# An interleaved attention and token-mixer kernel: the last key block in two widths of columns, a query product moved into attention, and new turn lists

## The chip, the cores and the metric

The kernel runs on one core of a Trainium2 chip. The metric is the device time of one execution in microseconds, as the median of several runs. A core has these engines: TensorE (PE in the profile: matmuls; its weight loads are shown apart as PEld), VectorE (DVE), ScalarE (ACT), GpSimd (POOL) and SyncE (SP, which here issues the DMAs). Each engine takes its instructions in the order in which the program lists them, and waits at an instruction until the data that it needs have been written by the others. Matmuls write to PSUM, eight banks of 2 KB in each of 128 partitions; the other data lie in SBUF.

## The reference

```python
def _A_ref(x, wq, wk, wv, wo):          # S=2048, D=512, H=32, Dh=16
    q = (x @ wq).reshape(B, S, H, Dh).transpose(0, 2, 1, 3)
    k = x @ wk                          # one head of keys and values for all
    v = x @ wv
    scores = jnp.einsum("bhqd,bkd->bhqk", q, k) * (Dh ** -0.5)
    p = _softmax(scores, axis=-1)
    o = jnp.einsum("bhqk,bkd->bhqd", p, v)
    return o.transpose(0, 2, 1, 3).reshape(B, S, H * Dh) @ wo

def _B_ref(x, w1, b1, w2, b2):          # F=1792, the MLP runs along the tokens
    h = _layernorm(x, axis=-1)
    u = _gelu(jnp.einsum("bsd,sf->bdf", h, w1) + b1)
    y = jnp.einsum("bdf,fs->bds", u, w2) + b2
    return y.transpose(0, 2, 1)

x = A_x
x = x + _A_ref(_layernorm(x), A_wq, A_wk, A_wv, A_wo)
x = x + _B_ref(_layernorm(x), B_w1, B_b1, B_w2, B_b2)
x = x + _A_ref(_layernorm(x), A_wq, A_wk, A_wv, A_wo)
x = x + _B_ref(_layernorm(x), B_w1, B_b1, B_w2, B_b2)
```

Everything is float32. Products that need the precision are made of pairs: a number is split into a rounded part (type fp32r, "high") and the rest ("low"), and three matmuls of such parts stand for one.

## The kernel before

The program runs the two layers, 0 and 1, one behind the other; each is an attention and a token MLP. The 2048 tokens are 16 tiles of 128 (`x0` to `x15`) and four blocks of 512 (`b` = 0 to 3, four tiles each).

**Attention** goes through 32 groups. A group is four heads for one block of 512 queries; in layer 1 groups 0 to 7 belong to block 2. The scores of a group are 32 pairs: a pair is 128 keys against two heads, two matmuls of 512 columns into one two-bank PSUM tile `sc` (L909), and then one exponential over 128x1024 on ScalarE (L919). There are three `sc` tiles; a pair's tile comes free when its exponential has read it. To free it earlier, VectorE can copy a pair out of PSUM first (L917), and ScalarE then reads the copy (`p<-p` instead of `p<-sc`); such a pair is called copied here. The sums (`acc`, L925) are the matmuls of the exponentials with the values, four small ones for a pair. Below, 9.13 means pair 13 of group 9. The names in the code count differently: `sc_9_6_2` is group 9, key tile 6 (of 16, of 128 keys each), heads 2 and 3, so pair 13.

What TensorE does in what order during attention is set by lists of numbers, the **turns** (`WHOLE`, `LONG`, `COPIED`, `QUAD`, `QUAD_TO_FOUR` and so on, near the head of the file). A positive number issues the scores of that many pairs, the tens digit 1 (12, 13) marking that the last of them is copied; a negative number issues sums, so many pairs of them; a zero issues the next piece of other work: half a query product, a quarter of an output projection (`po`) or a product of the next MLP's first layer (`pu`). Work lies in a list that `later` makes (query products of later blocks, and the rows of their shifts), and in the Mixer, whose `turn` chooses lists for `po` and `pu`. A query product that finds enough room is given as a LONG turn of 16 pairs, otherwise as a WHOLE one of 12, so that what is put into the list early shifts where each later one falls. A **guard** (`proj.guard`, L627 in the profile) reads a flag, computed from bounds, and branches to a slow path that these data do not take; there is one in front of some groups, at which the engines stop for the branch.

**The entry of layer 1** is the code at the end of `tile_mqa_mixer_kernel`, behind layer 0's MLP, where no attention runs on any engine yet. `x` of the last block (tiles 12 to 15) is ready last. Its normalized tiles `h` are transposed by TensorE into `pt` (L386), split into high and low parts `hT` by ScalarE (`first_rows`, L397) and VectorE (`second_rows`, L401), and multiplied with the key and value weights into `pk` and, for block 2's queries, with `wq` into `pq` (both L415: `product` makes the generator of 12 matmuls, and `fill` issues so many of them). From `pk` come the squares `kk` (L457), `kg` (L449) and `kv` (L466) on ScalarE; from the squares, by a matmul with a column of ones (`pn`, L499), a maximum (`km`, L569), a diagonal (L571) and a matmul of that with ones (L573), the bound `kb` of the keys' norms (L576). It goes into row 0 of the keys, `kst`, in pieces (`bound_row`, L583), and the first scores need it. Each product of queries is put away in four steps: rounded (`round_queries`, L516, on ScalarE or VectorE), squared on GpSimd (`square_queries`, L524), subtracted to get the low part (`second_queries`, L528, VectorE), and stored to DRAM (`store_queries`, L533), from where the groups load it as `qs` (L788). `first_guard` issues the guard ahead of group 0; behind it `put` puts queries away between two steps of `bound_rows`, which writes the bound into the rest of `kst`.

In layer 1, before, the first three of block 2's four query products (0, 1, 2) are made in the entry, and only the fourth is left to `later`, as `project(NB - 2, [ND - 1])`.

## Time and profile before

| | us |
|---|---|
| median of 3 runs | 2517.36 |
| their lowest and highest | 2516.68, 2517.88 |
| the profiled execution | 2514.03 |
| its span in the trace | 2512.3 |
| PE busy | 2492.7 |
| ACT busy | 2102.8 |
| DVE busy | 1550.9 |
| POOL busy | 147.8 |

The page is of one execution. A row of its groups reads: line, engine, operation, out<-in with the tile's sizes and type, how many, then the busy time of all, the mean in ns of one, and the idle time of the engine ahead of them with what ended most of it. A row of the timeline begins with the start in us from the span's start and the time that the instructions of the row took together; in brackets stands the idle time ahead and what ended it. A row of the windows has a stretch, its length, the busy time of the engines asked for (instructions in brackets), the clock that TensorE was granted as a share of the full one, the share of the DMA engines' time and GB/s. Layer 0's exponentials run from 44.6 us to about 1041, layer 1's from 1296.3 to about 2289.

### The profile page before, as it was taken

To read this page: it belongs to the slowest core of one execution; us is meant where nothing else is said; L and a number is where in the kernel's file an instruction comes from. 1 tells how busy PE (TensorE), PEld (TensorE's weight loads), DVE (VectorE), ACT (ScalarE), POOL (GpSimd) and SP (SyncE) were. 2 spreads that over 40 slices of the span, in tenths; PEclk is the share of its full clock that TensorE was granted. 3 is DMA by queue.
4 is the path that set the end of the run, shared out by engine and by line. 5 is a ranking of instruction groups with operands and counts; after the bars stand their busy time and mean duration, and the time that the engine had idled before them with its cause. 6 is when DMAs were issued, how large, how long until landed. Compare 5 with 4: busy or idle time off the path is not lost. (4 is left out here: it accounts for less than half of the span.)

```text
span 2512.3 us, 41954 instructions
## 1 busy us (share of the span) xinstructions
PE 2492.7 (99%) x16158; PEld 1240.3 (49%) x16158; DVE 1550.9 (62%) x2458; ACT 2102.8 (84%) x2344; POOL 147.8 (6%) x235
## 2 busy tenths in 40 slices
PE   9999999999999999999999999999999999999999
PEld 6444334444444444588863443344444444445887
DVE  6565566667766776564445664666677667765522
ACT  6999999999999999653349999999999999995511
POOL 5000000000000000141000000000000000002200
PEclk9999999999999999999999999999999999999999
DMA  3221201111111111134423211111111111102343
GB/s 116 75 66 41 65 27 41 31 42 31 39 31 39 31 41 31 43 110 149 128 58 118 61 45 48 31 39 31 41 31 39 31 42 33 40 26 66 107 125 95
DMA packets 168679, 143.56 MB, mean 57 GB/s; under 512 B 17650, under 2 KB 132368, under 8 KB 167952
## 3 DMA queue, kind: packets, MB, share of 16 engines
q1 hardware_dynamic: 168464, 140.72, 19.3%
q8 instruction: 132, 2.16, 0.4%
q14 instruction: 83, 0.68, 0.1%
HBM read 97.67 MB, written 26.22 MB: 49 GB/s over the span
## 5 line engine op out<-in xcount | busy, mean ns | idle before, releaser
L919 ACT ACTIVATE p<-sc 128x1024 f32<-128x1024 f32 x1444 | 1404.4, 1048 | 62.6 <-PE sc L909 61.9
L917 DVE COPY p<-sc 128x1024 f32<-128x1024 f32 x604 | 739.1, 1224 | 520.8 <-PE sc L909 436.8
L925 PE MATMUL acc<-p,vaug 128*32 128x512 f32 x8192 | 999.3, 599 | 0.5 <-DVE q L528 0.5
L909 PE MATMUL sc<-qs,kst 51*128 51x512 f32 x4096 | 684.9, 432 | 10.2 <-ACT p L919 3.3
L919 ACT ACTIVATE p<-p 128x1024 f32<-128x1024 f32 x604 | 654.8, 1084 | 16.4 <-DVE p L917 11.0
L909 PEld LDWEIGHTS sc<-qs,kst 51*128 51x128 f32 x4096 | 338.1, 184 | 564.3 <-ACT p L919 393.8
L925 PEld LDWEIGHTS acc<-p,vaug 128*32 128x32 f32 x8192 | 218.8, 109 | 488.7 <-issue 472.5
L1455 PE MATMUL py<-u,w 128*128 128x512 f32 x1344 | 307.4, 390 | 0.0
L1455 PEld LDWEIGHTS py<-u,w 128*128 128x128 f32 x1344 | 251.9, 188 | 52.3
L1443 ACT CAST w<-w2r 128x896 fp32r<-128x896 f32 x64 | 60.3, 945 | 184.9 <-PE py L1455 177.3
L1202 PE MATMUL pu<-hb,w 128*128 128x512 f32 x792 | 209.6, 406 | 0.0
L1202 PEld LDWEIGHTS pu<-hb,w 128*128 128x128 f32 x792 | 140.9, 188 | 57.6 <-issue 31.1
L1189 POOL TENSOR_TENSOR w<-w1r,w 128x256 fp32r<-128x256 f32 x86 | 69.7, 818 | 1586.1 <-ACT w L1187 1584.0
L1444 DVE TENSOR_TENSOR w<-w2r,w 128x896 fp32r<-128x896 f32 x64 | 71.9, 1123 | 111.5 <-ACT w L1443 111.2
L845 DVE RECIPROCAL o<-o 128x128 f32<-128x128 f32 x120 | 113.3, 944 | 8.7 <-DMA o<-ev 8.7
L886 PE MATMUL po<-wo,hl 128*128 128x512 f32 x360 | 100.3, 412 | 0.1
L827 DVE COPY ev<-acc 128x512 f32<-128x512 f32 x64 | 43.7, 683 | 69.1 <-PE acc L925 69.1
L415 PE MATMUL pq<-hT,wq 128*128 128x512 f32 x312 | 81.1, 404 | 0.0
L886 PEld LDWEIGHTS po<-wo,hl 128*128 128x128 f32 x360 | 62.6, 188 | 33.6 <-issue 15.9
L1202 PE MATMUL pu_l<-hb,w 128*128 128x512 f32 x336 | 77.1, 389 | 0.0
L1461 DVE SCALAR_TENSOR_TENSOR x<-py,b2c,x 128x512 f32<-128x512 f32 x32 | 24.0, 750 | 81.2 <-PE py L1455 81.2
L1187 ACT CAST w<-w1r 128x256 fp32r<-128x256 f32 x86 | 34.4, 406 | 47.2 <-PE pu_l L1202 12.8
(191 smaller groups left out, 1179.3 us busy)
## 6 DMA issues: line engine op xcount, KB each, us to landing
w1r<-in_B_w_dram SPq DMA_DIRECT2D x224, 128.0 KB
w2r<-in_B_w_dram SPq DMA_DIRECT2D x64, 448.0 KB
qs<-qd SPq DMA_DIRECT2D x384, 64.0 KB
qd<-q SPq DMA_DIRECT2D x64, 256.0 KB
o<-ev SPq DMA_DIRECT2D x128, 128.0 KB
x<-in_A_x_dram SPq DMA_DIRECT2D x16, 256.0 KB
hd<-hT SPq DMA_DIRECT2D x2, 2048.0 KB
out_dram<-x SPq DMA_DIRECT2D x16, 256.0 KB
```

The costliest lines, as they stand in the source:

```text
L415: yield nc.tensor.matmul(out, a, c, start=(k == 0), stop=(k == len(terms) - 1))
L845: nc.vector.reciprocal(o[:, 1, c], o[:, 1, c])
L886: nc.tensor.matmul(po, a, c, start=(k == 0), stop=(k == 3 * len(parts) - 1))
L909: nc.tensor.matmul(sc[:, j, :], kst[kt // 4][rows, kt % 4 * P : (kt % 4 + 1) * P], qs[i % NQ][rows, j0 // 2, :], start=True, stop=True,)
L917: nc.vector.tensor_copy(pt, sc)
L919: nc.scalar.activation(pt, sc, AF.Exp, scale=0.25)
L925: nc.tensor.matmul(self.acc[i][c : c + 32, :], vaug[:, kt].rearrange("p d k -> p (d k)"), pt[:, j, :], start=(kt == 0), stop=(kt == NKT - ...
L1189: eng.tensor_tensor(w[:, 1], raw, f32(w[:, 0]), op=ALU.subtract)
L1202: nc.tensor.matmul(pu, a, c, start=(start and k == 0), stop=(stop and k == 5))
L1443: nc.scalar.copy(w[:, 0], raw)
L1444: nc.vector.tensor_tensor(w[:, 1], raw, f32(w[:, 0]), op=ALU.subtract)
L1455: nc.tensor.matmul(py, a, d, start=(c == 0 and f == 0 and k == 0), stop=(c == 1 and f == NFH - 1 and k == 2),)
```

## The change

Four things are changed.

In the entry, the last block's keys are made by two products: `three` over the 384 columns of tiles 12 to 14 and `one` over the 128 of tile 15, 12 matmuls each, into the same PSUM bank. Tiles 14 and 15 have their rows split in two steps, and three matmuls of `three` stand ahead of tile 15's transposes. The third query product of block 2 is taken out, together with its rounding, subtraction, squares and store. GpSimd's squares of the second product are issued behind the first two pieces of the bound's row instead of ahead of them.

`later` gets that third product: `project(NB - 2, range(2, ND))` gives two products instead of one.

`QUAD_TO_FOUR` has other numbers, and where the Mixer put `first` and `second` into a COPIED turn it uses a new list `ENTRY`. Both concern groups 8 to 10 of both layers.

```diff
--- before.py
+++ after.py
@@ -42,7 +42,10 @@
     13, -4, 13, 0, 0, 13, -4, 13, -4, 13, -4, 13, 0, 13, -4, 13, -4, 12, 0, 13, -4, 13, -4,
 )
 QUAD = (13, -4, 13, 0, 3, -6, 13, 0, 13, -4, 3, -4, 12, 0, 13, 0, 13, -6, 13, -4, 13, -4)
-QUAD_TO_FOUR = (3, -2) + QUAD[2:]
+QUAD_TO_FOUR = (
+    2, -2, 13, 0, 13, -4, 13, 0, 13, -4, 3, -6, 13, 0, 13, 0, 3, -6, 13, -4, 3, -4,
+)
+ENTRY = (1, 0, 13, 0, 13, -4, 13, -4, 13, -4, 13, -4)
 FOURS = (3, -4, 12, 0, 13, 0, -4, 3, -4, 12, 0, 13, -4, 0)
 SHORT = (2, 0, 3, -4, 3, -4)
 TINY = (2, 0, 2, -4)
@@ -406,11 +409,11 @@
             b = NB - 1
             self.hT[b] = self.pool2.tile([P, ND, 2, QB], F32R, tag="hT", name=f"hT{self.l}_{b}")
 
-        def product(self, out, weights, b):
-
-            hT = self.hT[b]
-            terms = [(a, hT[:, kt, 0, :]) for kt in range(ND) for a in weights(kt)]
-            terms += [(weights(kt)[0], hT[:, kt, 1, :]) for kt in range(ND)]
+        def product(self, out, weights, b, cols=slice(0, QB)):
+
+            hT, out = self.hT[b], out[:, cols]
+            terms = [(a, hT[:, kt, 0, cols]) for kt in range(ND) for a in weights(kt)]
+            terms += [(weights(kt)[0], hT[:, kt, 1, cols]) for kt in range(ND)]
             for k, (a, c) in enumerate(terms):
                 yield nc.tensor.matmul(out, a, c, start=(k == 0), stop=(k == len(terms) - 1))
 
@@ -442,6 +445,15 @@
             self.fill(self.halves[b], 2 * ND)
             self.pk[b] = pk
 
+        def last_keys(self, *columns):
+
+            b = NB - 1
+            pk = self.pk[b] = bank(b, f"pk{self.l}_{b}")
+            return [
+                self.product(pk, lambda kt: (self.wkv[:, 2 * kt, :], self.wkv[:, 2 * kt + 1, :]), b, c)
+                for c in columns
+            ]
+
         def key_rows(self, b):
             n, p = self.l, self.pool
             pk = self.pk[b]
@@ -673,7 +685,7 @@
                     rows(b)
             else:
                 att.weights()
-                project(NB - 2, [ND - 1])
+                project(NB - 2, range(2, ND))
                 then(-1, lambda: self.fetch(0))
                 rows(NB - 2)
                 project(0, range(2, ND))
@@ -1055,8 +1067,8 @@
                             continue
                         if self.pieces:
                             self.pieces.pop(0)()
-                        elif turn in (LONG, COPIED, DOUBLE, QUAD, QUAD_TO_FOUR, FOURS, WHOLE):
-                            room = 2.4 if turn in (COPIED, QUAD, QUAD_TO_FOUR) else 1.0
+                        elif turn in (LONG, COPIED, ENTRY, DOUBLE, QUAD, QUAD_TO_FOUR, FOURS, WHOLE):
+                            room = 2.4 if turn in (COPIED, ENTRY, QUAD, QUAD_TO_FOUR) else 1.0
                             mix.step(min(room, 0.8 * self.to_boundary()), self)
                         elif end:
                             mix.step(2.0, self)
@@ -1253,7 +1265,7 @@
             if early and (self.ready(KEPT + 1, 2) or self.last_pair_behind()):
                 return DOUBLE, [first, second] * 2
             even = not att.spares or att.to_boundary() in (14, 30)
-            return (COPIED, [first, second]) if even and self.ready(KEPT) else (PLAIN, [])
+            return (ENTRY, [first, second]) if even and self.ready(KEPT) else (PLAIN, [])
 
         def projection(self, att, which):
 
@@ -1652,47 +1664,46 @@
             proj.norm(tiles(b)[3:], (False,))
             two_, end = tiles(b)[:2], tiles(b)[2:]
             proj.transposes(two_)
-            pt = proj.pt[end[0]] = bank2(f"pt1_{end[0]}")
+            pt = bank2(f"pt1_{end[0]}")
+            proj.pt.update({end[0]: pt[:, :1, :], end[1]: pt[:, 1:, :]})
             proj.transpose(end[0], pt[:, 0, :])
             proj.first_rows(two_)
+            proj.first_rows(end[:1])
+            proj.fill(proj.queries(b - 1, 0, bank(0, f"pq1_{b - 1}_0")))
+            three, one = proj.last_keys(slice(0, 3 * P), slice(3 * P, QB))
+            proj.fill(three, 3)
+            proj.transpose(end[1], pt[:, 1, :])
             proj.second_rows(two_)
-            proj.fill(proj.queries(b - 1, 0, bank(0, f"pq1_{b - 1}_0")))
-            proj.transpose(end[1], pt[:, 1, :])
-            proj.first_rows(end)
-            proj.second_rows(end)
+            proj.first_rows(end[1:])
+            proj.second_rows(end[:1])
+            proj.second_rows(end[1:])
             proj.put_queries(b - 1, 0, True)
+            proj.fill(three, 5)
             second = proj.queries(b - 1, 1)
-            proj.fill(second, 5)
-            proj.keys(b)
+            proj.fill(second, 3)
+            proj.fill(three)
+            proj.fill(one)
             proj.last_squares()
             proj.key_rows(b)
             proj.key_copy(b)
             proj.fill(second, 4)
             pn = bank2(f"pn1_{b}")[:, 0, :]
             proj.norm_columns(b, pn)
-            proj.fill(second)
-            proj.round_queries(b - 1, 1, True)
-            proj.square_queries(b - 1, 1)
-            third = proj.queries(b - 1, 2, bank(0, f"pq1_{b - 1}_2"))
-            proj.fill(third, 2)
+            proj.fill(second, 2)
             bound = proj.key_bound(pn[:, None, :4], pn[:, P : 2 * P])
             next(bound)
             next(bound)
-            proj.fill(third, 7)
+            proj.fill(second)
+            proj.round_queries(b - 1, 1, True)
             next(bound)
             proj.bound_row(0, 0, QB // 2)
+            proj.square_queries(b - 1, 1)
             proj.second_queries(b - 1, 1)
             proj.flag()
             proj.key_split(b)
             att = Attention(1)
             att.begin()
-            proj.fill(third)
-
-            def put():
-                proj.store_queries(b - 1, 1)
-                proj.put_queries(b - 1, 2)
-
-            proj.first_guard(att, put)
+            proj.first_guard(att, lambda: proj.store_queries(b - 1, 1))
 
 
 # ---- launch: one core; inputs and outputs as the reference has them ----
```

How this moves instructions on TensorE shows at three places. The first is the entry of layer 1. Before, between the first query product of block 2 and the branch (`pt_14` is the transposes of tiles 14 and 15, `pk_3` the last block's keys, `pq_2_0` to `pq_2_2` the query products, `pn` the matmul of the diagonal and ones; where rows are left out, the four one-column matmuls of the squares stand):

```order
L415 MATMUL pq_2_0_13158<-hT_2_12884,wq_11890 128x512 x12
L386 MATMUL pt_14_13151<-ident,h_14_13077 128x128 x4
L415 MATMUL pq_2_1_13184<-hT_2_12884,wq_11890 128x512 x5
L415 MATMUL pk_3_13190<-hT_3_13128,wkv_11895 128x512 x12
L415 MATMUL pq_2_1_13184<-hT_2_12884,wq_11890 128x512 x4
...
L415 MATMUL pq_2_1_13184<-hT_2_12884,wq_11890 128x512 x3
L415 MATMUL pq_2_2_13225<-hT_2_12884,wq_11890 128x512 x2
L573 MATMUL pn_3_13213<-diag_13053,ones_12016 128x128
L415 MATMUL pq_2_2_13225<-hT_2_12884,wq_11890 128x512 x7
L909 MATMUL sc_0_0_0_13254<-qs_89,kst_84 128x512 x2
L909 MATMUL sc_0_0_2_13259<-qs_89,kst_84 128x512 x2
L415 MATMUL pq_2_2_13225<-hT_2_12884,wq_11890 128x512 x3
```

After:

```order
L418 MATMUL pq_2_0_13158<-hT_2_12884,wq_11890 128x512 x12
L418 MATMUL pk_3_13171<-hT_3_13128,wkv_11895 128x384 x3
L389 MATMUL pt_14_13151<-ident,h_14_13077 128x128 x4
L418 MATMUL pk_3_13171<-hT_3_13128,wkv_11895 128x384 x5
L418 MATMUL pq_2_1_13195<-hT_2_12884,wq_11890 128x512 x3
L418 MATMUL pk_3_13171<-hT_3_13128,wkv_11895 128x384 x4
L418 MATMUL pk_3_13171<-hT_3_13128,wkv_11895 128x128 x12
L418 MATMUL pq_2_1_13195<-hT_2_12884,wq_11890 128x512 x4
...
L418 MATMUL pq_2_1_13195<-hT_2_12884,wq_11890 128x512 x2
L585 MATMUL pn_3_13225<-diag_13053,ones_12016 128x128
L418 MATMUL pq_2_1_13195<-hT_2_12884,wq_11890 128x512 x3
L921 MATMUL sc_0_0_0_13258<-qs_89,kst_84 128x512 x2
```

The keys begin ahead of tile 15's transposes and no longer in one piece; two query matmuls instead of five stand in front of the ones matmul, and nothing of `pq_2_2` is left.

The second is the end of group 0 in layer 1, where the other work of the list stands between scores. Before, `pq_2_3` (the fourth product) has just been finished, and the four `pc` are the sums of the squares of block 2:

```order
L909 MATMUL sc_0_14_0_13726<-qs_89,kst_87 128x512 x2
L909 MATMUL sc_0_14_2_13731<-qs_89,kst_87 128x512 x2
...
L549 MATMUL pc_2_13736<-sq_2_0_13179,sel 32x512
...
L549 MATMUL pc_2_13736<-sq_2_1_13223,sel 32x512
...
L549 MATMUL pc_2_13736<-sq_2_2_13482,sel 32x512
...
L549 MATMUL pc_2_13736<-sq_2_3_13694,sel 32x512
L909 MATMUL sc_0_15_0_13744<-qs_89,kst_87 128x512 x2
L909 MATMUL sc_0_15_2_13749<-qs_89,kst_87 128x512 x2
L925 MATMUL acc_0_13524<-p_0_13_0_13710,vaug 32x512 x2
```

After, the product that has just been finished there is the third one, and the fourth follows:

```order
L921 MATMUL sc_0_14_2_13723<-qs_89,kst_87 128x512 x2
L921 MATMUL sc_0_15_0_13728<-qs_89,kst_87 128x512 x2
L418 MATMUL pq_2_3_13734<-hT_2_12884,wq_11890 128x512 x12
L921 MATMUL sc_0_15_2_13749<-qs_89,kst_87 128x512 x2
L921 MATMUL sc_1_0_0_13754<-qs_90,kst_84 128x512 x2
L921 MATMUL sc_1_0_2_13759<-qs_90,kst_84 128x512 x2
L937 MATMUL acc_0_13518<-p_0_13_0_13702,vaug 32x512 x2
```

The fourth product's twelve matmuls stand in one piece between the scores of pairs 30 and 31, where the `pc` stood, and every later product of groups 1 to 7 falls into another turn.

The third is group 8 of layer 1, pairs 17 to 23 (`sc_8_8_2` to `sc_8_11_2`); layer 0 has the same order there. The rows of `po` between them are left out. Before:

```order
L909 MATMUL sc_8_8_2_16539<-qs_89,kst_86 128x512 x2
L909 MATMUL sc_8_9_0_16544<-qs_89,kst_86 128x512 x2
L909 MATMUL sc_8_9_2_16549<-qs_89,kst_86 128x512 x2
...
L909 MATMUL sc_8_10_0_16563<-qs_89,kst_86 128x512 x2
L909 MATMUL sc_8_10_2_16568<-qs_89,kst_86 128x512 x2
L909 MATMUL sc_8_11_0_16573<-qs_89,kst_86 128x512 x2
L925 MATMUL acc_8_16428<-p_8_7_0_16523,vaug 32x512 x2
L925 MATMUL acc_8_16428<-p_8_7_2_16528,vaug 32x512 x2
L925 MATMUL acc_8_16428<-p_8_8_0_16533,vaug 32x512 x2
L925 MATMUL acc_8_16428<-p_8_8_2_16542,vaug 32x512 x2
L925 MATMUL acc_8_16428<-p_8_9_0_16547,vaug 32x512 x2
L925 MATMUL acc_8_16428<-p_8_9_2_16552,vaug 32x512 x2
```

After, from pair 16 on:

```order
L921 MATMUL sc_8_8_0_16551<-qs_89,kst_86 128x512 x2
L921 MATMUL sc_8_8_2_16556<-qs_89,kst_86 128x512 x2
L921 MATMUL sc_8_9_0_16561<-qs_89,kst_86 128x512 x2
...
L921 MATMUL sc_8_9_2_16575<-qs_89,kst_86 128x512 x2
L921 MATMUL sc_8_10_0_16580<-qs_89,kst_86 128x512 x2
L921 MATMUL sc_8_10_2_16585<-qs_89,kst_86 128x512 x2
L937 MATMUL acc_8_16445<-p_8_7_0_16540,vaug 32x512 x2
L937 MATMUL acc_8_16445<-p_8_7_2_16545,vaug 32x512 x2
L937 MATMUL acc_8_16445<-p_8_8_0_16554,vaug 32x512 x2
L937 MATMUL acc_8_16445<-p_8_8_2_16559,vaug 32x512 x2
L921 MATMUL sc_8_11_0_16599<-qs_89,kst_86 128x512 x2
```

Before, six pairs' sums follow in one piece and the next scores stand behind them; now there are four. Which of the pairs are copied moves too: before, 8.19, 8.25, 8.28, 9.1, 9.4, 9.7, 9.10, 9.13, 9.24, 9.26, 9.29, 10.0 and 10.8; now 8.18, 8.21, 8.24, 8.27, 9.1, 9.4, 9.10, 9.25, 9.28, 9.31, 10.2, 10.5 and 10.8. From the scores of pair 10.6 on both orders agree.

## The prediction

> **What bounds the kernel now.** I read the page's head, its busy times and its costliest groups first.
>
> ```profile
> span 2512.3 us, 41954 instructions
> PE 2492.7 (99%) x16158; PEld 1240.3 (49%) x16158; DVE 1550.9 (62%) x2458; ACT 2102.8 (84%) x2344; POOL 147.8 (6%) x235
> L919 ACT ACTIVATE p<-sc 128x1024 f32<-128x1024 f32 x1444 | 1404.4, 1048 | 62.6 <-PE sc L909 61.9
> L917 DVE COPY p<-sc 128x1024 f32<-128x1024 f32 x604 | 739.1, 1224 | 520.8 <-PE sc L909 436.8
> L919 ACT ACTIVATE p<-p 128x1024 f32<-128x1024 f32 x604 | 654.8, 1084 | 16.4 <-DVE p L917 11.0
> ```
>
> TensorE reads 99% busy, but its ends are modelled. What paces attention is ScalarE: 2048 exponentials, 604 of them on a score pair that VectorE has first copied out of PSUM. Their idle time (62.6 us, ended by scores) is what a better order can win. So I counted the exponentials that begin in stretches cut at one exponential's start. The view below gives, for each stretch, its length and ScalarE's busy time; one more is counted than begins there, since the one from before still ends inside.
>
> ```profile
> 1310.55:1326.06 15.51, 15.06 (x16) 1.00 0.39 143
> 1384.41:1396.53 12.12, 11.17 (x14) 1.00 0.37 98
> 1412.01:1425.00 12.99, 11.29 (x13) 1.00 0.29 78
> 1526.62:1541.19 14.57, 14.57 (x16) 1.00 0.27 74
> 1541.19:1549.55 8.36, 7.53 (x9) 1.00 0.09 25
> 1562.30:1620.51 58.21, 55.44 (x61) 1.00 0.10 29
> 1620.51:1651.31 30.80, 29.77 (x33) 1.00 0.14 40
> 314.92:373.43 58.51, 55.54 (x60) 1.00 0.09 28
> 373.43:403.98 30.55, 29.77 (x33) 1.00 0.14 41
> ```
>
> The fourth row is attention with nothing beside it: 16 exponentials in 14.57 us, 0.911 each, ScalarE never idle. That is my floor; a turn's **price** is its length less 0.911 for each exponential. The first row is a LONG turn (16 exponentials, one query product of twelve matmuls): 15.51 − 14.57 = 0.94. The second is a WHOLE turn (12, one product): 12.12 − 10.93 = 1.19. The third is a WHOLE turn that also holds a guard of the flag: 12.99 − 10.93 = 2.06. The fifth is the end of group 7 (8 exponentials and a guard, no product): 8.36 − 7.29 = 1.07.
>
> **Part 1, layer 1's entry.** Here nothing overlaps: all is one chain from the last transposes to the first scores. The timeline of before:
>
> ```profile
> 1282.36 1.47 PE L386 MATMUL pt<-ident,h 128*128 128x128 f32 x12
> 1283.58 3.01 PE L415 MATMUL pq<-hT,wq 128*128 128x512 f32 x12
> 1288.67 3.01 PE L415 MATMUL pk<-hT,wkv 128*128 128x512 f32 x12
> 1291.78 0.60 ACT L457 ACTIVATE kk<-pk 128x512 bf16<-128x512 f32 x1 [2.68 <-PE pk L415]
> 1292.55 1.40 PE L415 MATMUL pq<-hT,wq 128*128 128x512 f32 x5
> 1292.92 0.35 DVE L571 SCALAR_TENSOR_TENSOR diag<-ident,km,diag 128x128 f32<-128x128 f32 x1
> 1293.79 0.38 PE L573 MATMUL pn<-diag,ones 128*128 128x128 f32 x2
> 1294.19 1.04 POOL L524 TENSOR_TENSOR sq<-q 128x512 bf16<-128x512 f32 x1 [3.97 <-ACT q L516]
> 1294.54 1.21 DVE L583 TENSOR_SCALAR kst<-kst,kb 1x256 fp32r<-1x256 f32 x2
> 1295.73 0.81 PE L909 MATMUL sc<-qs,kst 51*128 51x512 f32 x4
> 1295.78 0.69 DVE L528 TENSOR_TENSOR q<-pq,q 128x512 fp32r<-128x512 f32 x1
> 1298.46 0.72 DVE L583 TENSOR_SCALAR kst<-kst,kb 1x256 fp32r<-1x256 f32 x2 [0.26 <-PEq L627]
> 1299.21 0.69 DVE L516 CAST q<-pq 128x512 fp32r<-128x512 f32 x1
> 1299.29 1.85 PE L909 MATMUL sc<-qs,kst 51*128 51x512 f32 x6 [1.86 <-DVE kst L583]
> 1301.06 0.20 PEld L925 LDWEIGHTS acc<-p,vaug 128*32 128x32 f32 x8 [0.65 <-DVE q L528]
> ```
>
> Twelve 512-column matmuls start 0.23 us apart (the rows start at 1283.58 and end 3.01 later, the last one's drain included); twelve of 128 columns take 1.47, 0.11 apart by the same reading. No row has 384 columns: three quarters of 0.23 is 0.17. So the last block's keys cost 12×0.17 + 12×0.11 = 3.4 us instead of 12×0.23 = 2.8, but the first eight 384-column ones now run before and after tile 15's transposes, on columns of tiles 12 to 14, while before TensorE ran five query matmuls there and the keys waited for tile 15's copies. Walking the new order with these spacings, and with the rows of the ScalarE and VectorE copies, the last key matmul starts draining near 1291.0 and the squares (`kk`) start at 1291.27 instead of 1291.78: **−0.51**.
>
> Second, the matmul by ones (L573) was ready at 1293.27 (diag, 1292.92 + 0.35) but stood behind five 512-column query matmuls until 1293.79. Only two are issued ahead of it now. With the half microsecond of above it runs at 1292.83: **−0.96** in all.
>
> Third, the two halves of the bound's row took 1.21 us beside GpSimd's square, and 0.72 where no square ran (1298.46). The square is now issued behind them: 0.49 less, so the first scores start near 1294.34: −1.39. What follows them is later by less: VectorE's L528 must wait for ScalarE's rounding of the second product, which ends near 1294.7, so it starts at 1294.75 instead of 1295.78, and flag, branch and the scores behind the branch come at 1298.26 instead of 1299.29: **−1.03**. Last, the third product's rounding (L516, 0.69 us) no longer stands in VectorE's queue ahead of its subtraction and the rows of keys that later scores need. The last row shows the first sums waiting 0.65 for that subtraction; without it they would wait a little less for their exponentials, so I count a third of L516's time: **−0.25**, chosen between nothing and 0.65. The entry's term, from the scores behind the branch on, is −1.03 − 0.25, **−1.25**. Its bounds: with 128-column matmuls at half their row's 0.11, −1.8; at the full 0.23 of 512 columns, twelve times 0.12 more, +0.2.
>
> On these 128-column matmuls a rule speaks. The Trainium skill, page "TensorE: Matmul & The Clock Gate", section "Back-to-back issue gap", states about 81 ns for each pair of weight load and matmul of 128 columns. By it the entry would be an estimated 0.35 better than by the row, whose transposes are 0.11 apart; the sum keeps the row.
>
> **Part 2, attention groups 0 to 7 of layer 1.** The third product of block 2 now runs among their turns. The turns change from 9 LONG, 2 WHOLE and 2 COPIED to 7 LONG, 5 WHOLE and 2 COPIED; the exponentials stay as many, four of them moving from plain stretches into turns. Two LONG go: −2×0.94 = −1.88. Three WHOLE come: 3×1.19 = +3.57. The guard that a WHOLE turn held (2.06 − 1.19 = 0.87 over its price) still has to be passed. Sum **+1.7**. TensorE spends 2.8 us more on the product there, but only what ScalarE waits for counts. Ends: one product at LONG's price and no other change, +0.94; every new WHOLE turn as dear as the one with the guard, 3×2.06 − 1.88 = +4.3. I take the undisturbed row, since two of the three new turns hold no guard. The third product's store and `qs` loads move by some microseconds; its group is read groups later, so that costs nothing, and would cost the store's delay only if the first loads of block 2 stood behind it.
>
> **Part 3, groups 8 to 10 of both layers.** 59 exponentials lie between the two places from which both orders agree. They take 58.21 and 58.51 us; at the steady pace of the 32 after them in layer 0 (30.55/32 = 0.955) they would take 56.3, so 1.9 and 2.2 are lost. Three stretches hold most of it:
>
> ```profile
> 1565.02:1571.50 6.48, 5.86 (x7) 1.00 0.00 0
> 1591.06:1594.65 3.59, 2.89 (x5) 1.00 0.00 0
> 1615.40:1617.73 2.33, 1.99 (x3) 1.00 0.03 7
> 1568.19 2.78 PE L925 MATMUL acc<-p,vaug 128*32 128x512 f32 x24
> 1570.90 0.96 PE L909 MATMUL sc<-qs,kst 51*128 51x512 f32 x6
> ```
>
> The first is six exponentials (8.17 to 8.22; 6.48 − 5.47 = 1.01 lost): three score pairs that are not copied, then sums of six pairs (24 matmuls, 2.78 us) before TensorE gives the next scores, and ScalarE has eaten its three by then. The second (0.86 lost) has a copy of pair 9.13 that stands behind normalization work on VectorE. The third (0.51 lost) follows three uncopied pairs, 10.1 to 10.3. In the new order the first pattern goes from 8.17 but comes back at 8.28 to 8.30 and, in part, at 9.5 to 9.7 (three uncopied, then six sums): −1.0 and +1.0, and up to +1.0 against a stretch that loses 0.88 already. Pair 9.13 isn't copied: −0.3 to −0.86. Pair 10.2 is: −0.5, and what stands at 10.5 instead is a copied pair in each batch, as in the steady part. I take −0.4 a layer, **−0.8**. Ends: all excess gone, −4.1; or a new stall of 0.6 a layer, +1.2.
>
> **Sum.** −1.25 + 1.7 − 0.8 = −0.35, made against the profiled execution, 2514.03 us (span 2512.3 and 1.7 around it), which lies 3.3 below the median of 2517.36. On the median it gives 2517.0: no change. A measurement of this kernel can tell about 0.2%, 5 us, from no change.
>
> **Rivals.**
>
> The turn lists do more (faster). If groups 8 to 10 come to the steady pace in both layers, −4.1 stands for −0.8: −3.65, 2513.7. For it: the copied pairs of 9.22 to 10.9 are spread evenly now. Against: two batches of three uncopied pairs with six sums stay. Chance 0.12.
>
> The narrow key matmuls are dear. The row of L573 above shows one matmul of 128 columns in plain fp32 as two records; if those of the keys took 0.22 as well, the entry would lose 12×0.11 = 1.3: +1.0, 2518.3. It decides from about 0.14 each, where the 0.35 is used up. Against: the transposes of the same width at 0.11. Chance 0.22.
>
> The whole products stall ScalarE (slower than before). A WHOLE turn issues its second half of six matmuls (1.4 us) in one piece behind the first; if ScalarE runs dry each time as in the turn with the guard, part 2 is +4.3: +2.25, 2519.6. It turns the sum positive from 1.31 us a turn, and would show as slower by 0.2% only from 3.0. Against: the turn without a guard. Chance 0.13.
>
> The clock falls again.
>
> ```profile
> 1296.00:1299.00 3.00, 1.43 (x7) 0.59 (x5) 2.15 (x8) 1.94 (x2) 0.00 (x0) 1.00 0.02 5
> 1299.00:1300.00 1.00, 0.71 (x3) 0.70 (x5) 0.94 (x3) 0.00 (x0) 0.02 (x1) 0.69 0.11 25
> 1300.00:1303.00 3.00, 3.00 (x15) 0.72 (x13) 2.91 (x6) 2.68 (x3) 1.02 (x1) 0.53 0.78 204
> 1300.32 2.85 ACT L919 ACTIVATE p<-sc 128x1024 f32<-128x1024 f32 x3 [2.03 <-PE sc L909]
> 1310.55 1.94 ACT L919 ACTIVATE p<-sc 128x1024 f32<-128x1024 f32 x2 [0.18 <-PE sc L909]
> ```
>
> After TensorE's idle time before 1299.29 the granted clock (the figure after the engines) is about half until 1303. Ten exponentials begin from 1300.32 up to 1310.55: 10.23 − 9.11, 1.1 us lost. The third product's last three matmuls (0.96 us) that ran in the gap go, and the idle time grows from 2.0 to about 3.2 us. If a second such stretch follows, +1.1: 2518.1. Chance 0.1. The Trainium skill's same page, "Part 1: The HAM clock gate (the "warmup" mystery)", puts the halving down to an idle window of about 3.4 us that runs free of the program; by that rule a longer gap makes the halved stretch likelier but not longer, and the sum would stay. The trace has one such stretch after a gap shorter than that.
>
> **How the numbers follow.** My forecast has the remaining chance, 0.43. Faster by over 0.2% needs the first rival and the best entry and more, slower by as much two of the others together: 0.03 and 0.04. The range runs from the first rival with the entry's better end (2513.7 − 0.55, 2513.2) to the third with part of the fourth (2520.4).
>
> **What would show it.** Right: `kk` near 1291.3, the ones matmul right behind diag, the bound's row at 0.72, the first scores 1.4 and those behind the branch 1.0 earlier; three more turns of 12 exponentials in about 12.1; groups 8 to 10 some 0.4 shorter. Wrong: key matmuls of 128 columns over 0.14 apart; ScalarE idle over 1 us in a product's turn; a change outside these three stretches, which my sum has at nothing because every other instruction is issued in the same order.

## The result and the profile after

The changed kernel took 2511.01 us (median of 13 runs, 2510.84 to 2513.63) against 2517.36 before (13 runs, 2514.59 to 2518.29): the ratio is 0.9979, with a 95% interval of 0.9971 to 0.9986, or 3.5 to 7.3 us less. The forecast was 2517.0 with a range from 2513.2 to 2520.4: too slow by 6 us, and the time lies below the range. The two profiled executions differ by less than the medians: 2514.03 before, 2511.45 after, spans 2512.3 and 2509.7. In the experiments two single executions, at granted clocks of 0.625 and 0.556 over the whole run, took 3552.17 and 3949.03 us, and the medians and ratios below leave them out.

The page's groups after, those that answer to the ones shown of before:

```profile
span 2509.7 us, 41974 instructions
L931 ACT ACTIVATE p<-sc 128x1024 f32<-128x1024 f32 x1441 | 1404.4, 1050 | 63.5 <-PE sc L921 62.7
L929 DVE COPY p<-sc 128x1024 f32<-128x1024 f32 x607 | 742.7, 1224 | 525.2 <-PE sc L921 439.6
L931 ACT ACTIVATE p<-p 128x1024 f32<-128x1024 f32 x607 | 659.4, 1086 | 12.9 <-DVE p L929 8.2
```

Three pairs more are copied; otherwise these rows tell little of where the time went: ScalarE's idle time ahead of its exponentials is 79.0 us before (62.6 + 16.4) and 76.4 now. It shows only when the span is cut at the same exponentials in both traces. Windows of before (stretch, length, ScalarE's busy time and instructions, granted clock, DMA share, GB/s); the first is from layer 0's last exponential to layer 1's first, then pairs 0.0 to 0.2, 0.2 to 0.12 and 0.12 to 8.14 of layer 1, and last the first twelve exponentials of layer 0:

```profile
1040.06:1296.35 256.29, 1.10 (x3) 1.00 0.37 108
1296.35:1300.32 3.97, 1.94 (x3) 0.88 0.04 10
1300.32:1310.55 10.23, 9.48 (x10) 0.88 0.70 201
1310.55:1562.30 251.75, 241.88 (x259) 1.00 0.24 70
44.58:57.37 12.79, 11.31 (x12) 1.00 0.29 76
```

The same stretches after, with 8.14 to 10.9 of layer 0 and of layer 1 ahead of the last:

```profile
1038.88:1293.94 255.06, 1.09 (x3) 1.00 0.36 108
1293.94:1297.88 3.94, 1.94 (x3) 0.81 0.04 10
1297.88:1309.33 11.45, 9.48 (x10) 0.77 0.54 173
1309.33:1562.56 253.23, 241.79 (x259) 1.00 0.24 70
315.82:372.23 56.41, 54.93 (x61) 1.00 0.10 30
1562.56:1618.92 56.36, 54.91 (x60) 1.00 0.10 29
44.55:58.29 13.74, 11.41 (x12) 0.88 0.26 70
```

Read as differences:

| stretch | before | after | change | forecast |
|---|---|---|---|---|
| entry, to 0.0 | 256.29 | 255.06 | −1.23 | −1.25 in all |
| 0.0 to 0.2 (the branch) | 3.97 | 3.94 | −0.03 | |
| 0.2 to 0.12 | 10.23 | 11.45 | +1.22 | a rival |
| 0.12 to 8.14 | 251.75 | 253.23 | +1.48 | +1.7 |
| 8.14 to 10.9, layer 0 | 58.51 | 56.41 | −2.10 | −0.4 |
| 8.14 to 10.9, layer 1 | 58.21 | 56.36 | −1.85 | −0.4 |
| 0.0 to 0.12, layer 0 | 12.79 | 13.74 | +0.95 | 0 |

These sum to −1.56; another −1.0 lies behind pair 10.9 of layer 1 and is taken up in the last section. Groups 8 to 10 gave 3.95 us instead of 0.8: in both layers their 59 exponentials now take 56.4, as long as at the steady pace of the 32 behind them (56.3). And +0.95 came in layer 0's first group, whose instructions are the same in both kernels; there the granted clock is 0.88 after and 1.00 before.

That last row is part of why the medians lie further apart than the traces: the profiled execution lies 3.3 us below its median before and 0.4 above it after. At the entries the clock falls to half for some microseconds, not in every execution. This is after, at layer 1's entry (after the length: busy time of PE, PEld, DVE, ACT and POOL, then the clock):

```profile
1294.00:1296.80 2.80, 0.13 (x1) 0.00 (x0) 2.34 (x9) 1.88 (x2) 0.70 (x1) 0.92 0.06 15
1296.80:1303.60 6.80, 6.75 (x30) 2.77 (x30) 3.10 (x8) 4.79 (x5) 0.00 (x0) 0.53 0.50 136
1303.60:1306.00 2.40, 2.40 (x20) 0.75 (x16) 0.00 (x0) 1.55 (x2) 0.00 (x0) 1.00 0.63 234
```

TensorE idles for 2.7 us at the branch, and its clock is then at half for 6.8 us, twice as long as in the trace of before. The execution of before that was profiled had one such stretch of 3.4 us and was among its fastest; the one profiled after had three in attention.

### The profile page after: what moved, and what is told of

Its sections match the earlier page's. It is cut to its first block, busy times and chain, and to the rows that moved or that the text cites. A ratio compares the mean times of both kernels' runs of the same rounds, so it can differ in the third digit from the quotient of the medians.

```text
span 2509.7 us, 41974 instructions
## 1 busy us (share of the span) xinstructions
PE 2493.1 (99%) x16170; PEld 1242.5 (50%) x16170; DVE 1554.8 (62%) x2462; ACT 2102.5 (84%) x2345; POOL 148.2 (6%) x235
## 5 line engine op out<-in xcount | busy, mean ns | idle before, releaser
L898 PEld LDWEIGHTS po<-wo,hl 128*128 128x128 f32 x360 | 62.6, 188 | 34.0 <-issue 16.4
```

The costliest lines, as they stand in the source:

```text
L898: nc.tensor.matmul(po, a, c, start=(k == 0), stop=(k == 3 * len(parts) - 1))
```

## The experiments

The theory now: the turn lists are worth about 4 us, the entry and the moved product together nothing, and how many halved stretches an execution meets spreads the times of one kernel over some 4 to 5 us. The rival: the lists' size is as forecast, and the entry gives more than its stretches show.

### The two halves of the change

The lists alone, on the kernel before:

```diff
-QUAD_TO_FOUR = (3, -2) + QUAD[2:]
+QUAD_TO_FOUR = (2, -2, 13, 0, 13, -4, 13, 0, 13, -4, 3, -6, 13, 0, 13, 0, 3, -6, 13, -4, 3, -4)
+ENTRY = (1, 0, 13, 0, 13, -4, 13, -4, 13, -4, 13, -4)
...
-            return (COPIED, [first, second]) if even and self.ready(KEPT) else (PLAIN, [])
+            return (ENTRY, [first, second]) if even and self.ready(KEPT) else (PLAIN, [])
```

> The kernel before with the new turn lists (QUAD_TO_FOUR, ENTRY) alone. The profile of the changed kernel has groups 8 to 10 shorter by 2.1 us in each layer. If the lists alone do that, this gives -4.2: 2513.1 against 2517.4. If the forecast's size (-0.4 a layer) was right and the rest came from the entry, it gives 2516.6.

It took 2512.12 (11 runs) against 2516.80 of before on the same chip, ratio 0.9984 (0.9975 to 0.9993): −4.0 by the ratio, with 1.8 to 6.3 as its interval. Stretch 8.14 to 10.9 of its two layers:

```profile
317.31:373.71 56.40, 54.91 (x60) 1.00 0.10 30
1562.41:1618.81 56.40, 54.93 (x61) 1.00 0.10 30
```

The rest alone, the changed kernel with the old lists:

```diff
-QUAD_TO_FOUR = (
-    2, -2, 13, 0, 13, -4, 13, 0, 13, -4, 3, -6, 13, 0, 13, 0, 3, -6, 13, -4, 3, -4,
-)
-ENTRY = (1, 0, 13, 0, 13, -4, 13, -4, 13, -4, 13, -4)
+QUAD_TO_FOUR = (3, -2) + QUAD[2:]
...
-            return (ENTRY, [first, second]) if even and self.ready(KEPT) else (PLAIN, [])
+            return (COPIED, [first, second]) if even and self.ready(KEPT) else (PLAIN, [])
```

> The changed kernel with the old turn lists: the new entry of layer 1 and the moved third product alone. If the parts add up and the lists are worth 4.2 of the 6.35, this gives -2.1: 2515.2. By the forecast's terms (-1.25 + 1.7) it gives 2517.8, and then something else than the sum of the parts makes the 6.35.

2515.09 against 2516.80 in the medians, but the ratio is 0.9998 (0.9989 to 1.0007): no difference. Its stretches: the entry, 0.2 to 0.12, 0.12 to 8.14, and 8.14 to 10.9 in layer 0:

```profile
1041.17:1296.26 255.09, 1.11 (x3) 1.00 0.36 108
1300.42:1310.80 10.38, 9.48 (x10) 0.86 0.65 191
1310.80:1563.82 253.02, 241.78 (x258) 1.00 0.24 70
316.07:374.54 58.47, 55.56 (x61) 1.00 0.10 28
```

So the entry's −1.2 is given back by the moved product's +1.3, about as the forecast had it, and no gain is left but that of the lists. This kernel's instructions at the entry are those of the changed kernel, yet ten exponentials took 10.38 here and 11.45 there: what follows the branch differs between executions.

### The two lists apart

On the kernel before, once with the new `QUAD_TO_FOUR` only and once with `ENTRY` only (each of the two edits of the first diff by itself). These two kernels, and the two of the next part, ran once each (2511.09, 2516.25, 2511.07 and 2512.02 us in their order here, before once in 2517.90); single times are not compared, only the stretches.

> The kernel before with the new QUAD_TO_FOUR alone (COPIED stays where ENTRY came). In the changed kernel's trace three waits of ScalarE that lie under this list are gone (at 8.23, 9.1 and 9.13, 1.83 us in all) and one is new (8.31, 0.53). If each list acts by itself, the stretch from 8.14 to 10.9 is 1.3 shorter in each layer: 57.2 in layer 0, 56.9 in layer 1. If the two act only together, because the pairs that are copied fall out of step at 9.22, it stays within 0.5 of 58.5 and 58.2.

> The kernel before with ENTRY alone (QUAD_TO_FOUR as before). By the traces it is worth the waits at 9.24, 9.26 and 10.6 (1.18 us) less the new one at 9.23 (0.64): 0.5 in each layer, 58.0 and 57.7 for the stretch from 8.14 to 10.9. If the two lists act only together: within 0.2 of 58.5 and 58.2.

Stretch 8.14 to 10.9 of both layers, with `QUAD_TO_FOUR` only:

```profile
316.49:373.45 56.96, 55.21 (x61) 1.00 0.10 29
1561.01:1617.93 56.92, 55.21 (x60) 1.00 0.10 29
```

With `ENTRY` only, and below it the same kernel's ten exponentials from 0.2 on:

```profile
318.19:375.84 57.65, 55.15 (x61) 1.00 0.10 29
1565.68:1623.34 57.66, 55.15 (x60) 1.00 0.10 29
1302.36:1313.93 11.57, 9.48 (x10) 0.76 0.69 217
```

−1.55 and −1.29 for the first, −0.86 and −0.55 for the second: each acts by itself, near what the waits in the trace gave (1.3 and 0.5), and together they are nearly their sum. The last row is the old entry with two halved stretches: they are not the new entry's alone.

### The entry's edits

The keys in one product of 512 columns again, in the changed kernel:

```diff
-            three, one = proj.last_keys(slice(0, 3 * P), slice(3 * P, QB))
-            proj.fill(three, 3)
...
-            proj.fill(three, 5)
             second = proj.queries(b - 1, 1)
-            proj.fill(second, 3)
-            proj.fill(three)
-            proj.fill(one)
+            proj.fill(second, 5)
+            (keys,) = proj.last_keys(slice(0, QB))
+            proj.fill(keys)
...
-            proj.fill(second, 2)
             bound = proj.key_bound(pn[:, None, :4], pn[:, P : 2 * P])
```

> The changed kernel with the last keys in one product of 512 columns behind tile 15's copies, five query matmuls ahead of it as before. The forecast gave the two widths 0.51 us. If that holds, the time from layer 0's last exponential to layer 1's first is 255.06 + 0.5 = 255.6; if the narrow matmuls cost what the early start wins, it stays at 255.06.

The square ahead of the bound's row again:

```diff
             proj.round_queries(b - 1, 1, True)
+            proj.square_queries(b - 1, 1)
             next(bound)
             proj.bound_row(0, 0, QB // 2)
-            proj.square_queries(b - 1, 1)
```

> The changed kernel with GpSimd's square of the second product issued ahead of the two pieces of the bound's row again. The forecast gave that order 0.49 us: layer 1's first exponential then comes at 255.55 behind layer 0's last instead of 255.06. The rival: in the new entry ScalarE rounds that product only after the two pieces (it ends at 1293.59, they end at 1293.35), so that the square cannot run beside them in either order, and it stays at 255.06.

The stretch up to layer 1's first exponential, with one key product:

```profile
1038.41:1293.70 255.29, 1.10 (x2) 1.00 0.37 108
```

With the square ahead, and from the same trace's timeline the bound's row, the rounding and the square:

```profile
1039.58:1294.66 255.08, 1.09 (x3) 1.00 0.36 108
1293.35 0.72 DVE L595 TENSOR_SCALAR kst<-kst,kb 1x256 fp32r<-1x256 f32 x2
1293.72 0.59 ACT L528 CAST q<-pq 128x512 fp32r<-128x512 f32 x1 [1.10 <-PE pq L418]
1294.38 1.04 POOL L536 TENSOR_TENSOR sq<-q 128x512 bf16<-128x512 f32 x1 [5.04 <-ACT q L528]
```

The two widths are worth 0.23 us, half of the forecast's 0.51. The order of the square is worth nothing (0.02): the bound's row takes its 0.72 with the square issued ahead as well, since ScalarE rounds the product only at 1293.72, and the square starts at 1294.38, when the row is done. What took the square away from the row, by this trace, is the rounding, which the new entry places behind the ones matmul. The other 1.0 of the 1.23 is left by difference: for the order of TensorE's work around the ones matmul, that rounding, and the split copies of tiles 14 and 15, with which `kk` is 0.16 earlier even where the keys are one product. No run parts these three.

### The idle time at the branch

The third product back in the entry, but in the gap behind the first scores, and one product fewer in attention:

```diff
-                project(NB - 2, range(2, ND))
+                project(NB - 2, [ND - 1])
...
             att.begin()
-            proj.first_guard(att, lambda: proj.store_queries(b - 1, 1))
+            third = proj.queries(b - 1, 2, bank(0, f"pq1_{b - 1}_2"))
+            proj.fill(third)
+
+            def put():
+                proj.store_queries(b - 1, 1)
+                proj.put_queries(b - 1, 2)
+
+            proj.first_guard(att, put)
```

> The changed kernel with the third product's twelve matmuls issued behind the first scores of layer 1, in TensorE's idle time at the branch (2.7 us in the profile), and put away in the guard as before; one product less in groups 0 to 7. If idle time there is what halves the clock a second time, that stretch (1.2 us) goes, and the product that leaves attention is worth 1.4: 2508.4. If the matmuls delay the branch and the copies on VectorE delay the keys, these give back 1 us or more: 2509.5 or above, with the halved clock no shorter.

2510.15 (nine runs), ratio to before 0.9975 (0.9965 to 0.9984). Its stretches 0.0 to 0.2, 0.2 to 0.12 and 0.12 to 8.14, and layer 0's first twelve exponentials:

```profile
1296.51:1300.93 4.42, 1.95 (x3) 1.00 0.10 23
1300.93:1310.69 9.76, 9.38 (x10) 1.00 0.67 171
1310.69:1562.37 251.68, 241.99 (x259) 1.00 0.24 71
45.40:60.87 15.47, 11.42 (x13) 0.78 0.24 63
```

Both effects are there: no halved clock at the entry (9.76 for 11.45) and the product's price gone from attention (251.68 for 253.23), against 0.48 for a later branch. Layer 0, the same code, met two halved stretches in this execution (15.47). On the changed kernel, whose ratio is 0.9979, no gain can be told. The next one moves four of the twelve matmuls behind the branch; beside it ran the changed kernel again, unchanged.

```diff
-            proj.fill(third)
+            proj.fill(third, 8)
...
                 proj.store_queries(b - 1, 1)
+                proj.fill(third)
                 proj.put_queries(b - 1, 2)
```

> As e2, but eight of the third product's matmuls ahead of the branch and four behind it, where TensorE waited 0.5 us for the keys. In e2 all twelve stood ahead and the branch came 0.9 later than it could. If that delay is what e2 paid (4.41 for 3.94 us from the first exponential to the third), this gives 3.9 to 4.0 there with no halved clock at the entry, 0.4 less than e2 in the profile's stretches and 2509 to 2510.5 in time. If TensorE is now idle long enough (about 1 us) for a halved stretch, 1.1 comes back behind it.

> The changed kernel, unchanged, on the same chip as e9, for a second profile. The time from the third to the thirteenth exponential of layer 1 was 11.45 with two halved stretches of the clock, and 10.38 with one in the kernel that has the same entry and the old lists. If that is chance, this run gives either of the two values, and groups 8 to 10 again 56.4 in both layers; if the number of halved stretches belongs to the kernel, it gives 11.4 again.

The first: 2511.82 (2508.50 to 2512.10), ratio 0.9976 (0.9967 to 0.9986). The changed kernel again: 2512.00 (2510.97 to 2514.92), 0.9982 (0.9973 to 0.9991). By medians these are not told apart, and the first missed the 2509 to 2510.5 that was expected. In the trace of the first (0.0 to 0.2, 0.2 to 0.12, and layer 0's first twelve), then of the second (layer 0's first twelve, 0.2 to 0.12):

```profile
1293.00:1297.08 4.08, 1.94 (x2) 1.00 0.04 10
1297.08:1306.81 9.73, 9.39 (x10) 1.00 0.66 180
44.41:57.29 12.88, 11.33 (x13) 1.00 0.29 75
```

```profile
45.26:60.79 15.53, 11.43 (x13) 0.78 0.24 62
1300.62:1311.55 10.93, 9.49 (x11) 0.81 0.63 181
```

Most of the later branch is won back (4.08 for 4.42), and the entry's clock stays full. The changed kernel's second profile took 1.8 us longer than its first in layer 0's first twelve exponentials and 0.5 less at 0.2, with two halved stretches in both: the same program differs by that much between executions. The kernel before, run again unchanged, gives the same picture:

> The kernel before, unchanged, for a second profile. The first has one stretch of half clock (1.7 us of clock lost, at 1300) and took 2514.03, 3.3 below the median; the changed kernel's has four (at 45, two at 1296, one at 2500). If stretches of half clock set the spread between executions, this profile, near the median, has several more, each some 0.9 to 1.2 long in ScalarE's pace. If not, it has one, and the 3 us lie elsewhere: in DMA waits or at the end.

Its ten runs have a ratio of 1.0002 (0.9993 to 1.0011) to the others of before. Its profiled execution took 2516.19 and had one stretch more than the first one of before, at layer 0's entry (13.88 for 12.79 us), besides one at layer 1's (10.56 for 10.23) and a first exponential that came 0.5 later. That is 1.9 of the 2.2 us between the two executions, so the expectation of "several more" was too many; only 1.4 of the 1.9 lie in stretches with a halved clock. The fourth stretch that it gives the changed kernel lies at the very end, where every profile has one.

Last, on top of the edit with eight and four matmuls, the gap at layer 0's branch filled with four that nothing reads:

```diff
+            "heat": lambda: heat(4, bank2("heat0")[:, 0, :]),
...
-    qmin k3 fds kk3 cdl pn2 kv3 pn3 pq4 kg3 diag fdl pnd pq5 kb row0 begin pq12 kst3 flag va0 wq2l
+    qmin k3 fds kk3 cdl pn2 kv3 pn3 pq4 kg3 diag fdl pnd pq5 kb row0 begin pq12 heat kst3 flag va0 wq2l
```

> As e9, with four more matmuls of 128 columns in plain fp32 (some 0.9 us; their result is read by nothing) in TensorE's idle time at layer 0's branch, which is 1.3 us long in e9. Eleven profiles of the same layer 0 entry show the first twelve exponentials in 12.8 to 15.6 us, with none to two halved stretches of the clock. If that idle time sets them off, this run has 12.8 to 13.0 there, and the times lose their upper cluster: a median near 2508.6, e9's lowest times. If the halved stretches come from what TensorE does behind the branch (waits of 0.4 us for VectorE), they still come in most executions, and the median stays near e9's 2511.8.

2509.03, and every run between 2508.91 and 2509.54; before on the same chip 2517.31, ratio 0.9969 (0.9957 to 0.9981). The trace, layer 0's first twelve exponentials and layer 1's 0.2 to 0.12:

```profile
44.64:58.04 13.40, 11.31 (x12) 1.00 0.28 72
1297.89:1307.62 9.73, 9.38 (x10) 1.00 0.70 181
```

The clock is full in both places. The four matmuls delay layer 0's branch by 0.5 us (13.40 for 12.88), and the upper cluster of times, 3 us higher, is gone. All six runs lie below the lowest of the 24 of the changed kernel (2510.84). Against before this is faster, by 0.2 to 0.4%; against the changed kernel the intervals of the two ratios still overlap (0.9971 to 0.9986 there). The run does not part the four matmuls' keeping TensorE busy from the 0.5 us by which they delay what follows.

## Why the prediction was wrong

**Part 3 was the step that failed.** It took −0.8 for groups 8 to 10; the trace and the lists alone give −3.95 and −4.0. The mechanism was right, waits of ScalarE at uncopied pairs and late copies, and its sizes in the new order were wrong. The text read 1.0 for "three score pairs that are not copied, then sums of six pairs" and let it come back in full at 8.28 to 8.30, with up to another 1.0 at 9.5 to 9.7. Here are ScalarE's rows of that first stretch before, and below them the pattern's return after:

```profile
1564.12 2.96 ACT L919 ACTIVATE p<-sc 128x1024 f32<-128x1024 f32 x3
1567.15 1.06 ACT L919 ACTIVATE p<-p 128x1024 f32<-128x1024 f32 x1
1568.12 2.83 ACT L919 ACTIVATE p<-sc 128x1024 f32<-128x1024 f32 x3
1571.50 1.03 ACT L919 ACTIVATE p<-sc 128x1024 f32<-128x1024 f32 x1 [0.56 <-PE sc L909]
```

```profile
1575.65 2.78 PE L937 MATMUL acc<-p,vaug 128*32 128x512 f32 x24
1575.73 2.89 ACT L931 ACTIVATE p<-sc 128x1024 f32<-128x1024 f32 x3
1578.36 0.96 PE L921 MATMUL sc<-qs,kst 51*128 51x512 f32 x6
1578.98 1.03 ACT L931 ACTIVATE p<-sc 128x1024 f32<-128x1024 f32 x1 [0.36 <-PE sc L921]
```

Before, the three exponentials from 1568.12 lose 3.38 − 3×0.911 = 0.65. The other 0.30 of the stretch stand ahead of the copied pair 8.19 (1567.15 − 1564.12 − 3×0.911), and that wait stays in the new order, ahead of 8.18. After, the three begin at 1575.73 and the next at 1578.98: 3.25 − 3×0.911 = 0.52. So the pattern was read as 1.0 where it cost 0.65 and came back as 0.52. At 9.8, where more was expected, ScalarE loses 0.50 after and lost 0.48 before (by the exponentials' starts), so nothing was added.

Step by step between the starts of layer 1's exponentials, the waits at 8.23, 9.1, 9.13, 9.24, 9.26 and 10.6 are gone (0.67, 0.35, 0.81, 0.29, 0.37 and 0.52), and those at 8.31 and 9.23 are new (0.53 and 0.64): −1.84 of the −1.85. The forecast had 9.13 and 10.6 in its sum, at −0.3 to −0.86 and −0.5; these two alone are −1.33, and it took −0.4 a layer because of the stall at 9.5 to 9.7 that did not come. The waits at 9.1, 9.23, 9.24 and 9.26 were not in its list; they make −0.37.

The first rival, "the steady pace in both layers", at −4.1 and a chance of 0.12, is what came in size. Part of that is luck: waits of 0.3 to 0.6 are still there, other ones than in the steady stretch, and they happen to add up to the same loss for each exponential.

**The base was the second.** The sum was made against the execution of 2514.03 and then put on the median, as if the 3.3 us between them stayed. The granted clock over each run tells most of where they lie: of the 33 runs of before beside the first experiments, three had 1.000 and took 2513.20 to 2513.83 us, ten had 0.999 and took 2514.06 to 2516.59, and twenty had 0.998 and took 2516.13 to 2518.21. One halved stretch of 3.41 us lowers that clock by 0.0007. So most runs met more such stretches than the profiled one. Counted without the extra ones after (0.95 in layer 0, 1.07 between 11.45 and the 10.38 of the same entry with the old lists), the trace's −2.58 becomes −4.6, inside the measured 3.5 to 7.3.

**A term put at nothing was not nothing.** Of the forecast's signs of being wrong one came clearly, "a change outside these three stretches": −1.0 behind pair 10.9 of layer 1, where the order is the same. Its cause stays open (last section).

**The entry came as forecast, for partly other reasons.** −1.23 to the first exponential and −1.26 to the third, for −1.25. `kk`, counted from the first transposes, is 0.45 earlier (0.51 forecast), though of that only 0.23 to 0.29 comes from the two widths; the ones matmul follows diag at once; the bound's row takes 0.72, but not through the order of the square. The −0.25 for the third product's rounding shows nowhere: the first sums behind the branch still wait 0.65, and in the run with the old lists, with one halved stretch as before, 0.2 to 0.12 takes 10.38 for 10.23. The −1.03 came as −1.26 instead. Between layer 0's last exponential and layer 1's third, the five profiles with the old entry differ by 0.7 among themselves, so the agreement to 0.01 is luck. (Two of the forecast's own additions are off a little: −1.03 − 0.25 is −1.28, and with the narrow matmuls at half their 0.11 the bound is −1.9, not −1.8.)

**The second rival fell.** The row of the last four 384-column and the twelve 128-column matmuls is this:

```profile
1287.82 2.25 PE L418 MATMUL pk<-hT,wkv 128*128 128x384 f32 x16
```

Less 4×0.17 that is 1.57 for twelve, its drain included; the transposes' row of before had 1.47. The spacing is that of the transposes, 0.11 by the single starts, and not the 81 ns of the Trainium skill's page "TensorE: Matmul & The Clock Gate" (section "Back-to-back issue gap").

**The moved product** cost 1.48 (253.23 − 251.75) for 1.7, and 1.3 with the old lists. The turns came as counted, 7 LONG and 5 WHOLE. Each of the five products in one piece costs ScalarE 1.1 us at one exponential's start, as the two of before do: the third rival, with 2.06 a turn, fell.

**The fourth rival came, in this execution,** at 1.2 us for 1.1, with TensorE idle for 2.7 us at the branch. Of five profiles with the new entry's gap four have a second halved stretch (10.93 to 11.52 us from 0.2 to 0.12, against 10.38); of five with the old entry one has two and one has none. That the longer gap makes it likelier fits this, but ten executions don't show it. With work in the gap none of three profiles has a halved stretch at this entry; of the ten without it nine have.

## What to carry to other kernels

When a profile is one execution, find out where in the range of the kernel's times it lies before a sum is put on the median. Count the stretches of lowered clock first: they are worth more here than most edits, and filling the wait at a branch with work that was due anyway, or with work that nobody reads, removed them in the profiles here. Where a hand-written order is replaced, list every wait of the stretch exponential by exponential, and price a pattern from its own rows, not from a stretch that holds another wait as well.

## What the runs showed of the hardware that was not expected

The clock falls to half after gaps in TensorE's work that are far shorter than the stretch that follows. At layer 0's branch TensorE is idle for 0.8 to 1.4 us and, in most profiles, for another 0.4 to 0.5 behind it; of twelve profiled executions with the same code there nine have one or two halved stretches, and four matmuls (1.16 us) in the first gap went with a full clock and six runs within 0.63 us of each other. The Trainium skill, page "TensorE: Matmul & The Clock Gate", section "Part 1: The HAM clock gate (the "warmup" mystery)", has the clock fall after an idle window of about 3.4 us: here 1.05 to 3.04 us of idle time in the 3.41 before the fall were enough. The length of one halved stretch, 3.41 us, agrees with that page.

Whether a gap does it depends on when it comes. Within one execution the halved stretches begin whole multiples of 3.413 us apart: after, at 47.10 and 1296.38, 366 of them; in the second profile of before at 49.13 and 1301.82, 367. Cut on that grid, layer 0's branch falls into two intervals before and into one after (the only engine here is TensorE, whose ends are modelled):

```profile
43.28:46.69 3.41, 2.40 (x10) 1.00 0.01 1
46.69:50.10 3.41, 2.72 (x18) 1.00 0.10 26
43.68:47.10 3.42, 2.23 (x10) 1.00 0.04 10
47.10:50.51 3.41, 3.41 (x16) 0.50 0.21 46
```

TensorE is idle for 1.01 and 0.69 us in the first two rows, of before, and the clock stays full; in the third, after, it is idle for 1.19, and the next interval has half the clock. In all thirteen traces, from 5 us on and up to the last 8, every such interval of full clock with 1.19 us or more of idle time is followed by half a clock (14), none with 1.01 or less is, and between 1.05 and 1.18 there are four that are and three that are not. So the same gap costs one execution about 1 us and another nothing. With the four matmuls at layer 0's branch no 3.41 us there hold more than 1.18 us of idle time, wherever the grid falls; without them up to 1.77. The first intervals of the program do not fit: up to 2.6 us idle there, and a full clock behind it.

Behind pair 10.9 layer 1 took 667.3 us before and 666.3 after, though the order is the same there. It is five single exponentials, each about 0.25 us later than after, at the same pairs in both profiles of before (10.12, 12.21, 22.17, 27.23 and 31.24), with a little given back elsewhere; in the second profile of the changed kernel none is late, and in the kernel with the lists alone three are (12.21, 19.14 and 31.24). So it belongs to the program and not to the execution; what it is was not tried and stays open.
